# How many weight pieces each pair of heads starts: one in the first two, two in the last two

## The chip, the cores and the metric

The kernel runs on one core of a Trainium2 chip. The metric is device time in microseconds of one execution. Three runs of the kernel before gave 914.96, 915.29 and 916.54 us; the median is 915.29. A further execution was profiled, and every duration below comes from it.

## The reference

Two blocks, one after the other. The first is attention with a hash mask; the second is a gated feed-forward block (SwiGLU) over the attention's output. Shapes: 4 batches, 8 heads, 768 positions, head size 64; then 3072 tokens of 512, and a hidden width of 1536.

```python
q_bits = (np.einsum('bhsd,dk->bhsk', q, proj) > 0)        # 6 bits; k likewise
mask = q_bucket[:, :, :, None] == k_bucket[:, :, None, :]
scores = np.where(mask, scale * q @ k.T, -1e9)
attn = softmax(scores)                                    # over the last axis
x = (attn @ v)  # (B,H,S,D) -> (B*S, H*D)
g = x @ w_gate;  silu = g / (1 + exp(-g))
out = (silu * (x @ w_val)) @ w_out
```

The three weight matrices come as 64-bit floating point numbers; the program sees them as pairs of 32-bit words.

## The kernel before, in words

**Attention.** The 32 heads are taken as 16 pairs (`pairs`), one after another, in the loop of L648. For pair n the loop issues 12 score units (`score`, L536: matmuls L523 into a PSUM tile, then the exponential L533 on ScalarE), the sums of the previous pair (`total`), the hashing of the next pair (`prepare_pair`), and then 12 `attend` units (matmuls L554 into the tile `av`). After the last of these ScalarE copies `av` out of PSUM (L560 and L561). Sums go through DRAM and come back broadcast: `row` (L595), `few` (L597), its reciprocal (L603), `sums` (L605), `r` (L612), and the product (`norm`, L619), about a pair and a half later.

**PSUM.** There is one pool, `pp`, of four tiles of two banks. Score tiles, `av`, the hashing and sum tile `joint`, and in the gated block the tiles `a`, `n` and `o` all come from it in turn. A matmul that takes the next tile waits until what was in it has been read out.

**Weight pieces.** The weights are needed as three 32-bit parts each, whose sum is the 64-bit value. The conversion is cut into 36 pieces of 128 partitions by 512 elements, numbered in the order in which the gated block wants them. A piece goes through these steps:

- `load_words` (L130): the DRAM to SBUF load of 512 KB into one of three `words` buffers;
- `scale` (L139, L140): two ScalarE instructions. Pieces 2i and 2i+1 share a stage tile, and the pool of stage tiles, `stagep`, has two buffers, so the `scale` of an even piece takes a buffer that the two pieces two tiles earlier held;
- `widths` (L153, L155, L158): three VectorE instructions, then the word load of a later piece;
- `round_up` (L146): one ScalarE instruction;
- `parts` (L166, L168): two VectorE instructions, then the write of the piece to DRAM (L170, 768 KB, `ram<-stage`), which frees its half of the stage tile.

In the attention loop, `begin_pieces(PACE[n])` (L677) rounds up the pieces whose widths are done and starts `PACE[n]` new ones, ahead of the `attend` units of pair n. `keep_pieces` (L684), behind the `attend` units, issues the parts of the pieces whose widths are done. `widen_pieces` (L656, and L687 after the last pair) issues the widths. So a piece started in pair n is widened at the start of pair n+1 and written at the end of pair n+1. Word loads and writes of this stage are issued on the queue of POOL, where the loads of finished weights (`bring`, L251, `ring<-ram`, from pair 13 on) stand too.

**Gated block.** Blocks of 1024 tokens; for each, 12 up steps (`U`, matmuls of gate and value into `a` and `n`, read by L752 and L758) and 4 down steps (`D`, into `o`, read by L813 to L819). Pieces that the attention has not started or finished are taken by `turns` (L221): each turn finishes the pieces already widened, then starts one more. Its steps are spread over the atoms of the first block by the loop of L923: one and then two, two, two in an up step. Here the writes and word loads go on SP's queue (L868), and `bring` stays on POOL's. A ring of six buffers holds the finished weights.

The order in which each engine works is the order of the program text: the schedule is written out by hand. Each engine runs its instructions in that order and waits where a semaphore says so.

Of the kernel before, what the change touches and what calls it, by code (L numbers as in the profile page):

```python
# [19 lines left out]
def kernel(  # L20
# [68 lines left out]
    def finish(todo):  # L89
        while todo:  # L90
            todo.pop(0)()
# [82 lines left out]
    def begin_pieces(count):  # L174
        for i in sorted(added - rounded):
            round_up(i)
        for i in range(progress["scaled"], min(progress["scaled"] + count, NPIECE)):
            load_words(i + 1)
            scale(i)
# [125 lines left out]
    def attention(scope):  # L305
# [328 lines left out]
        def settle():  # L634
            while waiting:
                last.append(waiting.pop(0)())
# [4 lines left out]
        load_words(3, nc.sync)  # L641
        steps = front(1)
        last = []
        PACE = [1, 2] + [2, 1] * 7
        splits = []
        later = []
        TURN = 5
        for n in range(len(pairs)):  # L648
# [26 lines left out]
            if not more:  # L675
                settle()
            begin_pieces(PACE[n])  # L677
            finish(splits)
# [17 lines left out]
    with ExitStack() as scope:  # L696
        attention(scope)
# [264 lines left out]
```

## Time and profile before

| | us |
|---|---|
| median of three runs | 915.29 |
| the profiled execution | 915.68 |
| its span, first to last instruction | 913.8 |
| TensorE matmuls busy | 903.9 (99%) |
| VectorE busy | 665.5 (73%) |
| ScalarE busy | 450.4 (49%) |
| POOL busy | 88.9 (10%) |
| attention, from the start to the first up matmul | 321.3 |
| gated block, from there to the end | 592.5 |

Busy is the time in which an engine had an instruction under way. A line of the profile's groups or timeline names the line of the kernel, the engine, the operation, and the tiles out<-in; in brackets stand the idle time before the instruction and what released it. PE is TensorE, PEld its weight load, ACT ScalarE, DVE VectorE, SP the sync engine. A name with q (POOLq, SPq) is the engine's queue of DMA issues. The chain is the work that ended last, followed back from the end step by step.

### The profile page before, as it was taken

How to read it: one execution, taken by the hardware profiler on the slowest of the kernel's cores; microseconds unless marked ns; L12 is line 12 of the kernel's file. 1: busy time of each engine (PE TensorE's matmuls, PEld its weight loads, DVE VectorE, ACT ScalarE, POOL GpSimd, SP SyncE). 2: the span in 40 equal slices, each digit the busy share in tenths (PEclk: the TensorE clock that was granted, in tenths of full speed). 3: DMA queues.
4: the chain of work that ended last, by engine and by line, in shares of the span. 5: the costliest groups of instructions: out<-in, count | busy, mean ns of one | idle time of the engine just before them, and what ended most of it. 6: DMA issues, size and time to landing. Idle time of an engine off the chain costs nothing.

```text
span 913.8 us, 12448 instructions
## 1 busy us (share of the span) xinstructions
PE 903.9 (99%) x4801; PEld 637.3 (70%) x4801; DVE 665.5 (73%) x783; ACT 450.4 (49%) x606; POOL 88.9 (10%) x178
## 2 busy tenths in 40 slices
PE   9998999999999999999999999999999999999998
PEld 4443444444444478788888888888888888888886
DVE  6786999999988858779785955365568754474746
ACT  7767888888887745542423133331313233313220
POOL 1010011000111120100001000101000100001000
PEclk9998999999999999999999999999999999999999
DMA  7576778878878499785756573433444642515332
GB/s 181 107 180 160 182 188 204 233 187 226 232 197 235 164 356 337 249 290 203 295 202 230 184 271 120 173 139 141 150 157 149 244 140 91 217 70 208 103 138 93
DMA packets 143706, 174.24 MB, mean 191 GB/s; under 512 B 103360, under 2 KB 113568, under 8 KB 143648
## 3 DMA queue, kind: packets, MB, share of 16 engines
q0 software_dynamic: 22384, 115.62, 35.4%
q1 hardware_dynamic: 119856, 56.64, 23.8%
q10 hardware_dynamic: 1408, 1.20, 0.5%
q8 instruction: 38, 0.62, 0.3%
q14 instruction: 20, 0.16, 0.1%
HBM read 133.17 MB, written 39.42 MB: 189 GB/s over the span
## 4 chain that ended last, share of the span: by engine, by line
PE 85%; DVE 6%; DMA 4%; ACT 2%; issue 2%; SPq 1%; ACTq 0%; DVEq 0%; POOLq 0%
PE a L713 25%; PE o L713 19%; PE sc L523 15%; PE n L713 13%; PE av L554 10%; DMA r<-sums 1%; DMA sums<-few 1%; DMA ram<-stage 1%; PE joint L590 1%; PE joint L431 1%; DVE v L758 1%; DVE v L762 1%; DVE g L758 1%; DVE hid L769 1%; DVE o L815 0%
## 5 line engine op out<-in xcount | busy, mean ns | idle before, releaser
L713 PE MATMUL a<-xparts,ring 128*128 128x512 f32 x1152 | 272.9, 389 | 0.0
L713 PEld LDWEIGHTS a<-xparts,ring 128*128 128x128 f32 x1152 | 216.2, 188 | 45.4 <-issue 0.6
L713 PE MATMUL o<-ring,hid 128*128 128x512 f32 (+1 forms) x870 | 198.4, 388 | 0.4 <-DVE o L819 0.4
L713 PEld LDWEIGHTS o<-ring,hid 128*128 128x128 f32 x870 | 162.8, 188 | 34.3 <-DVE o L819 0.8
L523 PE MATMUL sc<-qT,kT 64*128 64x384 f32 x768 | 154.8, 489 | 4.9 <-ACT xT L561 4.7
L533 ACT ACTIVATE A<-sc 128x768 f32<-128x768 f32 x192 | 153.6, 816 | 2.0 <-PE sc L523 1.2
L713 PE MATMUL n<-xparts,ring 128*128 128x512 f32 x576 | 142.2, 389 | 0.0
L554 PE MATMUL av<-A,vraw 128*64 128x386 f32 (+1 forms) x768 | 127.7, 488 | 0.0
L713 PEld LDWEIGHTS n<-xparts,ring 128*128 128x128 f32 x576 | 108.1, 188 | 22.4
L758 DVE TENSOR_TENSOR v<-v,n 128x1024 f32<-128x1024 f32 x36 | 44.0, 1222 | 97.4 <-PE n L713 93.0
L251 POOL DMA_DIRECT2D ring<-ram x108 | 56.9, 529 | 498.8 <-PE n L713 322.3
L554 PEld LDWEIGHTS av<-A,vraw 128*64 128x64 f32 x768 | 53.7, 136 | 73.3 <-issue 62.8
L523 PEld LDWEIGHTS sc<-qT,kT 64*128 64x128 f32 x768 | 69.0, 189 | 46.8 <-issue 34.5
L752 ACT ACTIVATE g<-a 128x1024 f32<-128x1024 f32 x36 | 36.9, 1025 | 129.7 <-PE a L713 129.0
L763 ACT ACTIVATE hid<-v 128x1024 fp32r<-128x1024 f32 x36 | 38.2, 1062 | 113.2 <-DVE v L762 110.6
L760 ACT ACTIVATE g<-g 128x1024 f32<-128x1024 f32 x36 | 38.2, 1061 | 90.3 <-DVE g L758 90.3
L819 DVE TENSOR_TENSOR o<-o 128x512 f32<-128x512 f32 x92 | 63.0, 687 | 18.9 <-ACT o L813 16.5
L758 DVE TENSOR_TENSOR g<-g,n 128x1024 f32<-128x1024 f32 x36 | 43.8, 1216 | 32.6 <-PE n L713 32.6
L523 PE MATMUL sc<-qb,kb 64*128 64x384 bf16 x384 | 63.2, 325 | 0.0
L572 DVE SCALAR_TENSOR_TENSOR both<-A 128x1536 f32<-128x1536 f32 x32 | 55.4, 1731 | 6.6 <-ACT A L533 5.1
L769 DVE SCALAR_TENSOR_TENSOR hid<-hid,v 128x1024 fp32r<-128x1024 f32 (+1 forms) x39 | 44.5, 1141 | 19.2 <-ACT hid L763 19.1
L576 DVE TENSOR_TENSOR both<-both,A 128x1536 f32<-128x1536 f32 x32 | 56.0, 1749 | 2.6 <-ACT A L533 1.1
(80 smaller groups left out, 692.8 us busy)
## 6 DMA issues: line engine op xcount, KB each, us to landing
ring<-ram POOLq DMA_DIRECT2D x108, 768.0 KB, 5.1
ram<-stage POOLq DMA_DIRECT2D x23, 768.0 KB, 4.3
ram<-stage SPq DMA_DIRECT2D x13, 768.0 KB
vraw<-in_v_dram SPq DMA_DIRECT2D x16, 384.0 KB
out_dram<-o SPq DMA_DIRECT2D x23, 256.0 KB
kraw<-in_k_dram SPq DMA_DIRECT2D x60, 96.0 KB
qraw<-in_q_dram SPq DMA_DIRECT2D x60, 96.0 KB
r<-sums SPq DMA_DIRECT2D x30, 192.0 KB
```

Of the source, the lines that this page charges most:

```text
L251: nc.gpsimd.dma_start(t.bitcast(FP32), ram[at].bitcast(FP32))
L523: nc.tensor.matmul(banks_of[u][:, h], x["k", n][rows, ks], x["q", n][rows, qs], start=start, stop=stop)
L533: nc.scalar.activation(weights(u)[:, :, 0:HQ], banks_of.pop(u), AF.Exp, scale=SCALE * (1.0 if units[u][0] else OFF / 2))
L554: nc.tensor.matmul(ps[h * D : (h + 1) * D, 0:width], raws["v", n][:, h, c, :], a[:, h, 0:width], start=c == 0, stop=c == NCH - 1)
L572: nc.vector.scalar_tensor_tensor(out=t, in0=first, scalar=S * EPS / P / 2, in1=now, op0=ALU.add, op1=ALU.add)
L576: nc.vector.tensor_tensor(t, t, now, op=ALU.add)
L713: nc.tensor.matmul(ps, w, x, start=start, stop=stop)
L758: nc.vector.tensor_tensor(two(z), two(z), n_, op=ALU.subtract)
L760: nc.scalar.activation(z, z, AF.Silu)
L763: nc.scalar.activation(h, val, AF.Copy, scale=TOWARD / STEP)
L769: nc.vector.scalar_tensor_tensor(out=l_, in0=h_.bitcast(FP32), scalar=-STEP, in1=v_, op0=ALU.mult, op1=ALU.add)
L819: nc.vector.tensor_tensor(accs[c], accs[c], t[:, 1], op=ALU.subtract)
```

## The change

The list of how many pieces each pair starts is another one.

```diff
-        PACE = [1, 2] + [2, 1] * 7
+        PACE = [1, 1] + [2, 1] * 6 + [2, 2]
```

Written out, by pair 0 to 15: before 1 2 2 1 2 1 2 1 2 1 2 1 2 1 2 1, after 1 1 2 1 2 1 2 1 2 1 2 1 2 1 2 2. Both sum to 24. Entries 1 and 15 differ. From piece 2 on the same place in the loop therefore works on a piece with a number lower by one, up to pair 15. There two pieces are started, and both are still to be rounded up, parted and written when the gated block begins; before it was one. The first turn of the gated block has nine steps instead of seven, and each later step comes two places later. No matmul and no transfer is added or removed; the stage tile that a piece falls into follows its number.

## The prediction

> **What bounds the kernel now.** I read the page's busy times first, then the waits of the stretch where TensorE stood idle, then the timelines of ScalarE and TensorE there, then the chain.
>
> ```profile
> PE 903.9 (99%) x4801; PEld 637.3 (70%) x4801; DVE 665.5 (73%) x783; ACT 450.4 (49%) x606; POOL 88.9 (10%) x178
> PEclk9998999999999999999999999999999999999999
> ```
>
> TensorE's matmuls leave 9.9 us of the span uncovered, and one slice (the fourth, 68.5 to 91.4 us) shows a lower granted clock. A change is worth what it does to those 9.9 us and to that slice. Of the 9.9 us about 1.0 is before the first matmul and 3.7 after the last; 0.4 is at 375 us; the rest is one gap. Its waits, from 46 to 77 us:
>
> ```profile
> ACT stage L139 <- DMA ram<-stage: 7.5, 1, 7.5
> ...
> PE sc L523 <- ACT xT L561: 4.7, 1, 4.7
> ```
>
> The timelines say who stood behind whom, ScalarE first, then TensorE (start, duration, what; in brackets the idle time before it and its releaser):
>
> ```profile
> 62.49 0.67 ACT L140 ACTIVATE words<-words 128x512 int32<-128x512 uint16 x1
> 70.61 0.68 ACT L139 ACTIVATE stage<-words 128x512 f32<-128x512 f32 x1 [7.45 <-DMA ram<-stage]
> 71.19 0.66 ACT L140 ACTIVATE words<-words 128x512 int32<-128x512 uint16 x1
> 71.75 0.14 ACT L560 ACTIVATE e<-av 128x1 f32<-128x1 f32 x1
> 71.81 0.77 ACT L561 COPY xT<-av 128x768 f32<-128x768 f32 x1
> ```
>
> ```profile
> 65.30 0.34 PE L523 MATMUL sc<-qb,kb 64*128 64x384 bf16 x2
> ...
> 67.57 0.33 PE L523 MATMUL sc<-qb,kb 64*128 64x384 bf16 x2
> 72.63 1.65 PE L523 MATMUL sc<-qT,kT 64*128 64x384 f32 x4 [4.73 <-ACT xT L561]
> ```
>
> In pair 2 `begin_pieces` starts pieces 3 and 4. Piece 4 opens the third stage tile of a pool of two, so its `scale` waits for the tile of pieces 0 and 1. Piece 1 was started in pair 1, widened at the start of pair 2, and its parts come on VectorE only at 64.9 to 67 us; the write to DRAM follows (issued at 66.9, landing after 3.6 us, at 70.5). ScalarE stands for 7.45 us, and behind it the copy of `av` (L561), which frees the PSUM tile that TensorE needs for the third score unit of pair 3.
>
> The price is read from the chain, where each pair's scores begin:
>
> ```profile
> 91.63 9.80 PE sc L523 x72
> 102.85 7.91 PE av L554 x48
> 110.76 9.79 PE sc L523 x72
> ```
>
> A pair takes 110.76 - 91.63 = 19.13 us; so did the one before the gap (46.17 to 65.30). From 65.30 to 91.63 are 26.33 us, so the gap costs 7.20 us. The window table accounts for it: after the gap TensorE works at half clock.
>
> ```profile
> 73.00:74.00 1.00, 1.00 (x4) 0.29 (x4) 0.44 (x2) 1.00 (x3) 0.41 (x1) 0.50 0.92 242
> ...
> 77.00:78.00 1.00, 1.00 (x10) 0.52 (x8) 0.25 (x1) 0.57 (x2) 0.00 (x0) 1.00 0.25 98
> ```
>
> (The number after the last parenthesis is the granted clock.) In finer windows the clock falls to 0.50 at about 70.1 us and is full again at 76.9. Of that, 72.63 to 76.9 is work at half speed: 4.2 us of which half, 2.1, is lost. Idle 4.73 + 2.1 = 6.8; the remaining 0.4 no row names. I take 7.20, the difference of starts, and 6.8 as the lower end.
>
> **What the Trainium skill says.** "TensorE: Matmul & The Clock Gate", Part 1 (What's actually happening), says that TensorE falls to half clock after an idle window of about 3.4 us and needs a busy one to come back. The trace agrees in kind: 0.50, fallen 2.4 us into the gap, back 4.2 us after work resumed; the 0.38 us gap at 375 us left the clock at 1.00. The same page (Architectural detail) says ScalarE and VectorE are strict first-in first-out: L560 and L561 indeed stood behind L139 although their data were ready at about 65.3. "DMA: Bandwidth & Descriptors", Issuing engines are not separate DMA queues, says that all transfers share the 16 engines whoever issues them. The trace agrees: one ring load of 768 KB lands in 4.7 us when issued at 349.1, in 15.9 us when issued at 327.3, where the DMA share is 1.0.
>
> **The change part by part.** The total stays 24 pieces. Pair 1 starts one instead of two; pairs 2 to 14 start the same counts, so every piece from number 2 on comes one place later; pair 15 starts two instead of one. One piece more is therefore unfinished when the gated block begins.
>
> Removed, pair 2: with piece numbers shifted, pair 2 starts 2 and 3, which open the second stage tile, never used before. Piece 4 comes in pair 3 (at about 81 us), and the writes of 0 and 1 were issued in pairs 1 and 2 and land by about 70: 10 us of margin. No wait, no gap, no half clock: -7.20.
>
> Removed, pair 1: one `scale` on ScalarE, two instructions of 0.58 us from start to start, and in pair 2 three widening steps (0.42 + 0.69 + 0.69) and two of the parts (0.68 + 0.69) on VectorE. Worth nothing: TensorE was not waiting there (ScalarE itself idled 1.60 us for `av` at 46.28).
>
> Later stage tiles: each even piece needs the piece two tiles back written. Counted through, the last of those was always kept at the end of the pair before, so about 10 us of margin with a write of about 4.3; for piece 22, in pair 15, about 6. Worth nothing, covered by TensorE's 19 us per pair. If one lacked cover it would rebuild the old gap.
>
> Added, pair 15: one more `scale` (2 x 0.58 us) on ScalarE before L560, which waited 5.15 us for TensorE at 320.65. Its words are issued at about 305.3 and land in about 7.5 us, before 315. Nothing. Three widening steps, 1.8 us of VectorE, come before the norm of pair 14, whose wait covers them:
>
> ```profile
> 331.08 1.02 DVE L619 SCALAR_TENSOR_TENSOR xT<-xT,e,r 128x768 f32<-128x768 f32 x1 [7.97 <-DMA r<-sums]
> ```
>
> Without that cover it would still have to eat 1.4 us of slack first (a PSUM tile freed at 336.35 and wanted at 337.76).
>
> Moved on POOL's queue: the second widening issues a second word load (512 KB) before three ring loads.
>
> ```profile
> 322.33 0.53 POOL L251 DMA_DIRECT2D ring<-ram  x1
> 323.41 0.53 POOL L130 DMA_DIRECT2D words<-in_moe_w_out_dram  x1 [0.55 <-DVE stage L158]
> 324.24 1.57 POOL L251 DMA_DIRECT2D ring<-ram  x3 [0.30 <-issue]
> ```
>
> The three go out 1.9 us later. The first of them now lands at 324.24 + 10.7 = 334.9; TensorE wants it at 337.76. Behind a full queue the extra 512 KB costs 512 KB / 331 GB/s = 1.6 us (336.5, slack 1.3); if the delay of issue adds to it, 338.4, a stall of 0.6. I take nothing and keep 0.6. The two after it have 6.0 and 8.3 us (landing 337.2 and 340.3, wanted 343.2 and 348.6). The load at 322.33 stays where it was (lands 331.7, wanted 332.32).
>
> Moved to SP's queue: one more 768 KB write in the first up step; SP waits there anyway, and the ring loads it competes with then have 10 us. The word load of piece 27 falls behind the wait for the sums (to about 352 instead of 340); piece 27 is scaled at about 368. Nothing.
>
> Moved on VectorE and ScalarE, first four up steps: the first turn of the gated block has nine steps instead of seven, so all later steps sit two places on. VectorE's round stays about 10.5 us (the `v` copy comes about 0.5 us earlier since `scale` now stands behind it, one widening step of 0.6 falls in after `hid`), against TensorE's 10.88. But at the first down step:
>
> ```profile
> 375.71 4.62 PE L713 MATMUL o<-ring,hid 128*128 128x512 f32 x19 [0.38 <-DVE o L819]
> ```
>
> That stall waits for the second L819, which now has one L155 (0.6 us) more in front of it. Cost +0.6 (0 to 1).
>
> Sum: -7.20 + 0.6 = -6.6. The profiled execution took 915.68 (span 913.8, 1.9 around it), so 909.1 and a span of 907.2; the median of the runs is 0.4 lower than the profiled one: 908.7.
>
> **The rivals.** First, late weights: the ring load above stalls TensorE by 1 to 2.5 us in the second up step, too briefly for the clock. For it: a DMA share of 1.0 to 1.03 from 328 to 348 us. Against: it had 2.8 us to spare and the queue is merely 1.6 us longer. Time 909.7 to 911.2.
>
> Second, on the other side: that same stall lasts past the point where the clock falls (2.4 us in the old gap). Then it costs its length plus 2.3. To eat 6.6 us it must last 4.3, so the load must land at 342.1, 7.2 us later than before; beyond, the kernel is slower, by some 2 us at 344. Against: nothing adds more than 3.5 us to it. Time 915 to 918.
>
> Third, the gap moves instead of going: piece 4 in pair 3 finds the write of piece 1 not landed. For it: the same two buffers and the same queue. Against: 10 us of margin where the old case had minus 8. Time 915, no change.
>
> **How the numbers follow.** Main case 0.79, at 908.7, own range 907.7 (no stall at 375 at all) to 909.4; late weights 0.13; long late weights 0.05; moved gap 0.03. The range reaches over the main case and most of the first rival: 907.6 to 910.8. A measurement of this kernel can tell about 0.2%, 1.8 us, from no change: faster is the first two cases, 0.92; same 0.03; slower 0.05.
>
> **What would show it.** Right: no wait of ScalarE for a stage write in pair 2, starts of scores 19.13 us apart from 46 us on, clock 1.00 throughout after the start, everything from pair 3 on about 7.2 us earlier. Term by term: the wait for L819 near 368.5 us reads about 1.0 instead of 0.38; the norm of pair 14 still waits, about 6 us, for its transfer. Wrong: a wait of TensorE on ring loads after the first up step, or a clock below 1.00 anywhere later.

## The result

The changed kernel takes 911.13 us (median of 6 runs, 909.58 to 911.90), the kernel before 915.86 beside it (6 runs, 914.96 to 916.54): ratio 0.9947, 95% interval 0.9935 to 0.9960. It is faster, as forecast, but by 4.7 us and not by 6.6 (forecast 908.7, range 907.6 to 910.8).

The profiled execution took 910.49 with a span of 908.7. Its page, busy times and granted clock:

```profile
PE 902.4 (99%) x4801; PEld 636.5 (70%) x4801; DVE 664.9 (73%) x783; ACT 451.5 (50%) x606; POOL 88.6 (10%) x177
PEclk9999999999999999999999999999999999999999
```

No slice is left with a lower clock. The gap is gone: ScalarE's timeline in pair 2, then TensorE's at the start of pair 3.

```profile
62.57 0.69 ACT L140 ACTIVATE words<-words 128x512 int32<-128x512 uint16 x1
63.15 0.69 ACT L139 ACTIVATE stage<-words 128x512 f32<-128x512 f32 x1
63.72 0.71 ACT L140 ACTIVATE words<-words 128x512 int32<-128x512 uint16 x1
66.03 0.17 ACT L560 ACTIVATE e<-av 128x1 f32<-128x1 f32 x1 [1.60 <-PE av L554]
66.09 0.79 ACT L561 COPY xT<-av 128x768 f32<-128x768 f32 x1
```

```profile
65.91 0.34 PE L523 MATMUL sc<-qb,kb 64*128 64x384 bf16 x2
...
68.18 0.33 PE L523 MATMUL sc<-qb,kb 64*128 64x384 bf16 x2
68.34 0.81 PE L523 MATMUL sc<-qT,kT 64*128 64x384 f32 x4
```

The second L139 starts 0.58 us after the L140 ahead of it, where it had waited 7.45; the copy L561 waits only for `av`; the third unit's float matmuls start 2.43 us after the pair's first matmul, where they had started 7.33 us after it.

The span is 5.1 us shorter than in the first profile of the kernel before. From the first scores to the first up matmul 7.1 us are gained. Given back are 1.1 from there to the end of the first down step, 0.6 at the beginning, where both programs are the same (first scores at 7.21 instead of 6.60), and 0.3 behind the first down step. What the change itself moved lies in the first down step. TensorE, ScalarE and VectorE there:

```profile
358.50 10.36 PE L713 MATMUL o<-ring,hid 128*128 128x512 f32 x45
369.86 6.85 PE L713 MATMUL o<-ring,hid 128*128 128x512 f32 x27 [1.00 <-DVE o L819]
```

```profile
370.44 0.63 ACT L146 ACTIVATE stage<-stage 128x512 fp32r<-128x512 f32 x1 [4.46 <-DVE stage L158]
370.97 0.58 ACT L813 ACTIVATE o<-o 128x512 f32<-128x512 f32 x1
```

```profile
368.52 0.68 DVE L155 SCALAR_TENSOR_TENSOR stage<-words,stage 128x512 int32<-128x512 int32 x1
369.12 0.68 DVE L819 TENSOR_TENSOR o<-o 128x512 f32<-128x512 f32 x1
369.72 0.68 DVE L158 CUSTOM_DVE_ANT_0 stage<-words,stage 128x1024 uint16<-128x1024 uint16 x1
371.58 0.69 DVE L819 TENSOR_TENSOR o<-o 128x512 f32<-128x512 f32 x1 [1.18 <-ACT o L813]
```

The wait for the second L819 is 1.00 instead of 0.38, as forecast. A second piece step, L158, stands before the third L819 too; ScalarE's `round_up` (L146) waits for that L158, and the read-out of the third chunk (L813) waits behind L146. Counted from its first matmul to the next up step, the down step takes 18.05 us; it took 17.01 before, and the down steps after it take 16.3 to 16.4, with no wait in the list.

### The profile page after: what moved, and what is told of

Read it like the earlier page. It is cut to its first block, busy times and chain, and to the rows that moved or that the text cites. A ratio compares the mean times of both kernels' runs of the same rounds, so it can differ in the third digit from the quotient of the medians.

```text
span 908.7 us, 12452 instructions
## 1 busy us (share of the span) xinstructions
PE 902.4 (99%) x4801; PEld 636.5 (70%) x4801; DVE 664.9 (73%) x783; ACT 451.5 (50%) x606; POOL 88.6 (10%) x177
## 4 chain that ended last, share of the span: by engine, by line
PE 58%; DVE 2%; ACT 1%; issue 1%; DMA 1%; DVEq 0%; ACTq 0%; SPq 0%
PE a L713 26%; PE o L713 20%; PE n L713 13%; DMA words<-in_moe_w_out_dram 1%; DVE hid L769 0%; DVE g L758 0%; ACT v L752 0%; DVE stage L155 0%; DVE v L762 0%; DVE v L758 0%; ACT hid L763 0%; DVE o L819 0%; DVE stage L158 0%; DVE hid L772 0%; ACT o L813 0%
## 5 line engine op out<-in xcount | busy, mean ns | idle before, releaser
L523 PE MATMUL sc<-qT,kT 64*128 64x384 f32 x768 | 152.8, 483 | 0.3 <-ACT qb L436 0.2
L758 DVE TENSOR_TENSOR v<-v,n 128x1024 f32<-128x1024 f32 x36 | 44.0, 1222 | 99.5 <-PE n L713 97.6
L819 DVE TENSOR_TENSOR o<-o 128x512 f32<-128x512 f32 x92 | 63.0, 686 | 19.2 <-ACT o L813 16.9
L758 DVE TENSOR_TENSOR g<-g,n 128x1024 f32<-128x1024 f32 x36 | 43.8, 1216 | 34.9 <-PE n L713 34.9
```

Of the source, the lines that this page charges most:

```text
L523: nc.tensor.matmul(banks_of[u][:, h], x["k", n][rows, ks], x["q", n][rows, qs], start=start, stop=stop)
L758: nc.vector.tensor_tensor(two(z), two(z), n_, op=ALU.subtract)
L819: nc.vector.tensor_tensor(accs[c], accs[c], t[:, 1], op=ALU.subtract)
```

## The experiments

The first four ask what gives back a part of the gap's gain: the order of VectorE's steps in the down step (theory A), or the added traffic (rival B). The gated block has 14 writes of pieces in the changed kernel and in first_alone, 13 in the kernel before and in last_alone.

### first_alone: only the first entry

```diff
-        PACE = [1, 2] + [2, 1] * 7
+        PACE = [1, 1] + [2, 1] * 7
```

> Only the first entry of the list is changed (pair 1 starts one piece, pair 15 one as before; 23 pieces start in the attention, 13 stay for the gated block). Theory A (order): the gap at 66 us goes (7.1 us), and since each turn of the gated block has seven steps again, VectorE's order in the first down step is that of the kernel before: one wait there of about 0.4 us, no second one. That is about 1.0 us less than the changed kernel, so 910.1 us. Rival B (traffic: the gains missing after the change go to the one further write and word load that the gated block has to carry): 14 writes remain for it as in the changed kernel, so 911.1 us. If the gap depends on pair 15 too, 915.9.

Measured 910.53 us (ratio 0.9936, 0.9923 to 0.9948). The gap is gone, and the first down step takes 17.15 us, nearly what it took before. With one piece fewer started there is one turn more, and it collides with the third down step:

```profile
467.52 6.41 PE L713 MATMUL o<-ring,hid 128*128 128x512 f32 x27 [0.41 <-DVE o L819]
```

That step takes 17.02 us, 0.70 more than in the other kernels. So the first entry alone gives the gap's gain, and the last entry is what lengthens the first down step. A holds for the first down step, as the traffic of 14 writes did not lengthen it; the time lies between the two forecasts (910.1 and 911.1) and settles nothing by itself.

### last_alone: only the last entry

```diff
-        PACE = [1, 2] + [2, 1] * 7
+        PACE = [1, 2] + [2, 1] * 6 + [2, 2]
```

> Only the last entry is changed (pair 1 starts two, pair 15 two; 25 pieces start in the attention). Theory A (order): the gap at 66 us stays in full with its half clock, and the first turn of nine steps brings the longer waits in the first down step, 1.4 us together instead of 0.4: 1.0 us slower than the kernel before, 916.9 us. Rival B (traffic): the gated block has 13 writes as in the kernel before, so 915.9 us, no change.

Measured 918.10 us (17 runs, 916.09 to 919.74); the ratio is 1.0023, 1.0016 to 1.0030, so slower by about 2.1 us, more than either forecast. The first down step takes 17.99 us, 0.98 more than before, as A has it. The list of waits has one that the kernel before does not have:

```profile
ACT stage L139 <- issue: 8.7, 1, 8.7
...
ACT stage L139 <- DMA ram<-stage: 7.4, 1, 7.4
```

The 7.4 is the old gap, with TensorE's 4.7 behind it. The 8.7 is the same thing again in pair 15: the 25th piece opens a stage tile whose old contents are just being written. The view names no releaser, but the `scale` starts at 323.79 us, and the write of the piece two tiles back, issued at 319.63, lands at 323.64. TensorE had no scores left to stop, but POOL's three ring loads went out at 327.60 instead of 324.24 us. The profiled execution, at 916.42, was the second fastest of the 17; what the late loads cost the others was not traced, so the cause of the last 1 us stays open.

### realigned and late_tail: moving VectorE's steps

```diff
-                for _ in range(((1, 2, 2, 2) if kind == "U" else (1, 2, 2) + (1,) * 9)[at]):
+                for _ in range(((1, 2, 2, 2 if n else 4) if kind == "U" else (1, 2, 2) + (1,) * 9)[at]):
```

> The changed kernel, with nine steps instead of seven spent in the first up step (four after its last atom), so that from the second up step on every step falls where it fell before the change. Theory A (order): the waits in the first down step return to 0.4 us, 1.0 us less than the changed kernel, 910.1 us; the two more steps, 1.4 us of VectorE in the first up step, cost nothing, as the tile they delay is wanted 2 us later. Rival B (traffic): nothing changes, 911.1 us.

Measured 911.00 us (0.9945, 0.9931 to 0.9958): as the changed kernel. The first down step takes 17.71 us; 0.34 was won of the 1.04.

```diff
                 tail = atom()
-                finish(tails)
+                if kind == "U" or at:
+                    finish(tails)
```

> The changed kernel, but in each down step the two instructions that finish the last hidden tile (L769, L772) come after the second chunk's L819 instead of between the first chunk's and the second's. Theory A (order): the second L819 no longer stands behind 2.4 us of VectorE work, so the wait of 1.0 us at the sixth chunk of the first down step goes, and with it most of what follows: 1.0 to 1.4 us less than the changed kernel, 909.7 to 910.1 us. Rival B (traffic): 911.1 us.

Measured 910.55 us (0.9942, 0.9930 to 0.9955), not to be told from the changed kernel. In its profile the wait at the sixth chunk is gone, and one of 1.65 us stands one chunk later; before that, TensorE waited for a ring load:

```profile
326.33 3.92 PE L713 MATMUL a<-xparts,ring 128*128 128x512 f32 x16 [0.83 <-DMA ring<-ram]
373.31 4.38 PE L713 MATMUL o<-ring,hid 128*128 128x512 f32 x18 [1.65 <-DVE o L819]
```

Both moves left the end of the down step where it was. Theory A falls in the form that only the place of a step counts. Two new ones follow. C: VectorE enters the gated block behind TensorE, since the norm of pair 14 waits for its transfer, and the down step waits out what is left. D: the first ring load of the second up step lands just in time and misses in some executions (here, though the program is that of the changed kernel up to that place).

### after_again, early_ring, skip_norm, first_early: what VectorE starts with

> The changed kernel once more, beside the next three. Theory C (VectorE enters the gated block about 5 us behind TensorE, because the norm of pair 14 waits for its transfer, and what it has not made up by the first down step is waited for there): the first down step takes 18.0 us again (16.3 without waits). Theory D (the first ring load of the second up step lands within a microsecond of its use and misses it in some executions): the time of the profiled execution differs from the other runs by what TensorE waits for that load, 0 to 1.3 us. Median 911.1 us.

Measured 911.25 us (0.9949, 0.9936 to 0.9963). In this profile the first down step takes 19.11 us:

```profile
367.01 2.36 PE L713 MATMUL o<-ring,hid 128*128 128x512 f32 x9 [0.42 <-DVE o L819]
370.60 6.85 PE L713 MATMUL o<-ring,hid 128*128 128x512 f32 x27 [1.24 <-DVE o L819]
```

One program, and the step differs by 1.06 us between two executions.

```diff
-            if n >= len(pairs) - 3:
+            if len(pairs) - 4 <= n < len(pairs) - 1:
                 bring()
```

> The changed kernel with the three ring loads of the attention one pair earlier (pairs 12 to 14 instead of 13 to 15), so that the first weights of the second up step are there long before. Theory D: no wait of TensorE on a ring load, 0.5 to 1 us less than the changed kernel, about 910.3 us, and less spread. Theory C adds: the transfer for the norm of pair 14 has one load of 768 KB less beside it; if it lands earlier, the first down step gets shorter by part of that. If neither holds, 911.1 us.

Measured 909.38 us (0.9931, 0.9919 to 0.9944), no wait on a ring load, runs from 908.84 to 910.37. The norm of pair 14 waits 3.96 us, and the first down step takes 17.13. From the first up matmul to the end of that step are 60.77 us; they were 61.74 and 62.99 in after and after_again, where no ring load was waited for either, so what the profile won is C's. In the changed kernel's first profile the norm waits 5.88:

```profile
324.32 1.02 DVE L619 SCALAR_TENSOR_TENSOR xT<-xT,e,r 128x768 f32<-128x768 f32 x1 [5.88 <-DMA r<-sums]
```

```diff
         total(len(pairs) - 1)()
-        finish(last)
+        last.clear()
+        nc.sync.dma_start(kept_x[pairs[-2]], xT[len(pairs) - 2])
```

> The changed kernel without the norm of pair 14 (that pair's x is stored without being divided by its sums; the transfers for it are still made), so that VectorE does not wait before the first up step. Theory C: VectorE's first instruction of the gated block comes at about 320.6 instead of 325.3 us, the first down step takes 16.3 to 16.6 instead of 18.0 us, and the kernel 909.5 us. Theory A in its old form (only the order of VectorE's steps inside the down step matters): the waits stay, 911.1 us.

Measured 910.60 us (0.9943, 0.9930 to 0.9955). VectorE's first instruction, then TensorE (line numbers are one higher here):

```profile
320.16 1.22 DVE L759 TENSOR_TENSOR g<-g,n 128x1024 f32<-128x1024 f32 x1 [1.90 <-PE n L714]
```

```profile
331.75 3.91 PE L714 MATMUL a<-xparts,ring 128*128 128x512 f32 x16 [0.73 <-issue]
...
359.07 16.48 PE L714 MATMUL o<-ring,hid 128*128 128x512 f32 x72
```

VectorE now waits for TensorE, and the whole down step runs through in 16.32 us, by TensorE alone. The turn of nine steps is still there. So C is shown: without the late norm there is nothing to wait for. The time fell less than that, as TensorE now stood 0.73 us at the second half of the second up step. That is the load that the prediction's first rival named: issued at 319.41, it took 12.3 us and landed at 331.7, and TensorE went on at 331.75.

first_early is the list of first_alone with the loads of early_ring.

> Only the first entry of the list changed, and the three ring loads one pair earlier. Theories C and D together: the first down step at 17.1 us or less as in the run with the first entry alone, no wait on a ring load, and the 0.7 us in the third down step stays: 909.6 us. If the ring loads are no cause, 910.5 us as with the first entry alone.

Measured 909.22 us (0.9929, 0.9916 to 0.9941). First down step 16.32, third 17.03.

C can be put in a number. Take VectorE's first instruction of the gated block (L758) and the end of the first down step, when the next up step starts:

| run | L758 starts | down step ends | difference | down step takes |
|---|---|---|---|---|
| before | 332.02 | 381.98 | 49.96 | 17.01 |
| first_alone | 325.19 | 375.15 | 49.96 | 17.15 |
| after | 325.26 | 376.54 | 51.28 | 18.05 |
| after_again | 326.00 | 377.29 | 51.29 | 19.11 |
| last_alone | 331.27 | 382.57 | 51.30 | 17.99 |
| late_tail | 326.24 | 377.52 | 51.28 | 18.43 |
| early_ring | 323.94 | 375.25 | 51.31 | 17.13 |

While the step is longer than 16.32, its end hangs on VectorE's start: 49.96 us after it with turns of seven steps, 51.3 with a first turn of nine, in spite of different waits in between. The profiles below agree (before_1 and before_2: 49.95 and 49.96; odd_pairs: 51.27). The number of writes does not matter: first_alone has 14 and last_alone 13. The reason is in VectorE's own timeline. From its first L758 to the end of the step its waits are put down to ScalarE (one of 0.35 us to a transfer) and none to TensorE, in before and in after; with the earlier start of earlier_ring, below, three of its waits there are for TensorE (1.97, 0.66 and 0.71 us).

The difference, 1.3 us, fits two piece steps (L155 and L158, 0.6 to 0.7 each). VectorE's three rounds from one L758 of the gate tile (`g`) to the next take 11.04, 10.39 and 10.38 us in the changed kernel instead of 10.48, 10.50 and 10.50, 0.3 more together. From the last of them to the end of the down step are 19.47 us instead of 18.48, 1.0 more. This explains late_tail (the same work before the same end) and realigned (51.00: the two steps went earlier on the same engine).

### odd_pairs, earlier_ring, and the kernel before twice more

```diff
-        PACE = [1, 2] + [2, 1] * 7
+        PACE = [1, 2] * 8
```

> Pieces per pair one and two by turns from the start (1, 2, 1, 2, ...): pair 1 keeps its two pieces, as before the change, but pair 2 starts one, so that piece 4, which opens the third stage tile, comes in pair 3. Theory E (the gap came of the stage tile that is opened in pair 2): no gap, pairs 19.13 us apart, and from pair 15 on the state is that of the changed kernel, so 911.1 us. Rival F (the gap came of the load of two pieces in pair 1): the gap stays, 915.8 us.

Measured 911.14 us (0.9945, 0.9931 to 0.9958). Pair 1 starts two pieces here, and there is no gap; the third unit's float matmuls in pair 3 follow without a wait, and the pairs' scores start 19.13 us apart:

```profile
68.36 0.81 PE L523 MATMUL sc<-qT,kT 64*128 64x384 f32 x4
```

E is shown, F falls. The gap hung on the stage tile opened in pair 2.

```diff
-            if n >= len(pairs) - 3:
+            if len(pairs) - 5 <= n < len(pairs) - 2:
                 bring()
```

> The changed kernel with the three ring loads two pairs earlier (pairs 11 to 13), so that pair 14 has none either. If what VectorE waits for before the gated block is the chain of transfers of the sums of pairs 13 and 14 among the ring loads, it starts there 0.5 to 1 us earlier again than with one pair (9.5 us after the first up matmul), the first down step takes 16.3 to 16.7 us, and the kernel 908.7 us. If only the load beside the last transfer counts, as with one pair: 909.4 us.

Measured 908.52 us (908.40 to 911.01; 0.9922, 0.9908 to 0.9935), the fastest of all, and 2.6 us under the changed kernel's first median as well as under odd_pairs, which ran beside it. The norm and VectorE's start, then the down step:

```profile
320.19 1.02 DVE L619 SCALAR_TENSOR_TENSOR xT<-xT,e,r 128x768 f32<-128x768 f32 x1 [2.80 <-DMA r<-sums]
321.13 1.22 DVE L758 TENSOR_TENSOR g<-g,n 128x1024 f32<-128x1024 f32 x1
```

```profile
358.62 16.48 PE L713 MATMUL o<-ring,hid 128*128 128x512 f32 x72
```

VectorE starts 6.2 us after the first up matmul (314.94), where 8.5 to 9 was expected and 10.46 and 11.70 measured in the changed kernel; the down step does not wait at all, with the turn of nine steps still in it. So the two steps more cost time only while VectorE starts late.

> The kernel before, profiled once more, to see what differs between executions of one program: the gap with its half clock (7.1 us in the first profile), the start of the first scores (6.6 to 7.3 us in the profiles so far) and VectorE's start in the gated block (10.7 us after the first up matmul). If the changed kernel's smaller gain is due to a lucky first profile, the gap here is shorter than 7.1 us, 6 to 6.5; if not, it is 7.1 again.

> The same as the run ahead of it, a third profile of the kernel before: gap 7.1 us if the first profile was typical, 6 to 6.5 if it was not.

Measured 917.08 and 916.32 us, one execution each. From the first scores to the first up matmul the three profiles of the kernel before take 314.71, 314.31 and 315.53 us, the changed kernel 307.59. So the gap costs 7.12, 6.72 and 7.94, 7.26 on the average: the first profile was typical there. In before_1 TensorE also waits for a ring load:

```profile
PE a L713 <- DMA ring<-ram: 1.0, 1, 1.0
PE o L713 <- DVE o L819: 0.6, 1, 0.6
```

The just-in-time load is thus no product of the change.

The sum can now be made from profiled executions, 916.36 us on the average of the three of the kernel before and 910.87 of the two of the changed kernel (after and after_again): 5.49 apart. The gap gives 7.26. The first four up steps and the first down step together take 60.66, 62.13 and 60.22 us in the three profiles (mean 61.00), and 61.74 and 62.99 in the two (mean 62.37): 1.37 given back. VectorE's start is no part of that, at 11.05 and 11.08 us after the first up matmul on the average. The beginning gives back 0.18 (first scores at 6.78 and 6.96 us), the time behind the first down step 0.29 (531.89 and 532.18), of which 0.2 falls after the last matmul; its cause was not looked for. The medians are 4.7, 4.6 and 4.8 us apart (the last with odd_pairs), not 5.5: the profiled executions lie on the average 0.5 above the medians of the kernel before (about 915.9) and 0.3 below those of the changed kernel (911.13 and 911.25).

## Why the prediction was wrong

**The gap: right.** Forecast 7.2, measured 7.26 over three profiles, with the stage tile as its cause (odd_pairs), and the clock at full afterwards. In the profile that the forecast used it was 7.12; the chain's 91.63 is a little late, as the first score matmul of pair 4 starts at 91.56. No later stage tile held ScalarE up in the changed kernel; that last_alone's 25th piece met one in pair 15 shows how close the rule was.

**The first entry's lighter pair 1, and the cover for pair 15's added work: right.** VectorE's added widths fitted into its wait for the norm, which still lasted 5.88 us in the first profile, about 6 as forecast.

**The first down step: the step that failed.** The term reads "+0.6 (0 to 1)": one L155 ahead of the second L819. The one wait it names was right (1.00 instead of 0.38), and so was the kind of cause, the order of VectorE's steps. What was wrong is that the rest of VectorE's added work counted as covered, with a round of about 10.5 us against TensorE's 10.88. VectorE starts about 5 us late, for the norm (4.6 us later than in skip_norm). At 0.4 us per up step four up steps make up some 1.5 us of that, an estimate from these rounds. So VectorE never catches up before the down step ends, and the end stays a fixed distance behind its start, 49.96 us before and 51.28 after. All of the nine-step turn is paid for: 1.3 us instead of 0.6, the L158 ahead of the third L819 included, with ScalarE's read-out queued behind L146. The averages of the profiles say 1.37. With an early start the same turn costs nothing (16.32 in earlier_ring).

**What this leaves.** Forecast and measurement are 1.9 us apart. The mis-sized term is 0.8 of it; 0.2 lies at the beginning and is no effect of the change; 0.3 lies behind the first down step, and its cause is open. Most of the rest, some 0.7, is the difference between profiled executions and medians. The forecast took one execution for the kernel: the wait of 0.38 is 0.60 in before_1 and absent in before_2, and the up steps and down step together scatter by 1.9 us over three profiles of the kernel before and by 1.25 between two of the changed one.

**Late weights: underrated.** The prediction counted the slack of 0.6 us at the load issued at 322.33 as safe because it did not move. It is missed in some executions with either order (0.83 in late_tail, 1.0 in before_1), but in neither profile of the changed kernel, so as a cause of the difference between the kernels it is not shown. The rival's own load landed 1.3 us later than before, counted from the first up matmul (14.95 us after it, at 329.75, instead of 13.61), near the forecast's 1.6, and in time; it was late once, with the norm left out (0.73 in skip_norm).

**The rivals that reverse the sign** did not occur: no later gap, no lower clock.

## What to carry to other kernels

When work shared by turns is shifted by one piece, count who opens each reused buffer and when its last reader was queued: the fault was a tile opened in the same pair as the write of its old contents. Where two engines pace each other at nearly the same round, check how far behind the one with the shorter round starts; a wait at the border of two stages is no cover if the margin per round cannot make it up before the next place where both meet. Then the cheapest gain may lie in the transfers at that border: three loads moved two pairs earlier gave some 2.6 us on top of the change.

## What the runs showed of the hardware that was not expected

The half clock came in stretches of 3.41 us. After the same gap of 4.7 to 4.8 us it lasted 6.83, 3.41 and 6.83 us in the three profiles of the kernel before and 3.41 in last_alone; the full clock ahead of it had lasted 64.85 us once and 68.27 three times, 19 and 20 times 3.41. It began 2.2, 4.9, 3.8 and 5.0 us after TensorE's last matmul (2.2 is what the prediction gives as 2.4). In before_1 work had already resumed (at 72.95) when the clock fell (at 73.05).

How much matmul work fell into the stretch that was ending fits this. In the first profile the stretch from 66.71 to 70.12 us had 1.19 us of it, and the clock fell. In before_1 the stretch from 66.22 to 69.64 had 1.97, and the clock stayed full for one stretch more, in which TensorE worked for 0.10 (the number after the comma is TensorE's busy time, the last but two the granted clock):

```profile
66.71:70.12 3.41, 1.19 (x10) 0.45 (x6) 3.34 (x6) 0.00 (x0) 1.11 (x2) 1.00 0.90 346
66.22:69.64 3.42, 1.97 (x16) 0.80 (x12) 3.38 (x6) 0.00 (x0) 1.11 (x2) 1.00 0.75 286
```

last_alone stayed full after a stretch with 1.81. So in the first profile the clock fell although no whole stretch had been idle, sooner than after the whole idle window that the prediction speaks of; where between 1.2 and 1.8 us the limit lies, and whether it is one of busy time, these four do not show.

The price of one and the same gap ran from 6.7 to 7.9 us (7.12, 6.72, 7.94 and, in last_alone, 6.71). The idle time and half of the work done at half clock make 6.89, 6.47, 7.72 and 6.45 of it; 0.2 to 0.3 us stay unnamed in each.

At the beginning the records give the full clock from 3.7 to 6.9 us on, by execution, and the first scores start at 6.60 to 7.35 us, in fourteen profiles whose programs are the same up to there.
